# Reloading three chunks' keys, an earlier mask, no unread products, held weights and a new cut of the output in a delta rule with two MoEs

## The chip, the cores and the metric

The kernel runs on one core of one Trainium2 chip. The metric is the time of one execution on the device in microseconds (us); less is better.

## The reference

Three stages follow one another. The first is a recurrence (a delta rule) over 768 time steps for each of 4 batches and 8 heads, with a state of 48 x 48:

```python
k_n = k / (norm(k) + 1e-6)
for t in range(S):
    y[t]  = q[t] @ state
    state = state + beta[t] * outer(k_n[t], v[t] - k_n[t] @ state)
```

Its result, transposed, is a matrix x of 3072 tokens by 384. Two dense layers with a gate (called MoEs in the code) come after it:

```python
h = x @ w_in;  x = (h * tanh(softplus(h))) @ w_out      # first
h = x @ w_in2; out = (h * clip(h + 3, 0, 6) / 6) @ w_out2  # second
```

w_in is 384 x 2048 and w_out 2048 x 384. All is float32.

## The kernel before, in words

**Tiling.** The recurrence is cut into 24 chunks of 32 time steps (`NS`, `C`). All 4 batches x 32 steps of a chunk lie on the 128 partitions. For each chunk the kernel transposes k and q on TensorE (`T_pe`, line 403), forms the matrices of products among its steps (`G_pe`, line 420, masked by VectorE in `G_ew`, `G_ew2`, lines 441 to 451, the first with a mask times beta from `beta_mask`, line 393), solves a triangular system (`quads`, line 575, for chunks 0 to 7; `substs`, line 654, for the rest, on VectorE), and then takes the serial step in `rec` (line 786): products with the state (`state_pe`, L719), the new values (`U_pe`, L729), the output (`MU_pe`, L739), and the state's update (`S_mm`, L769, added by VectorE at L781). In the plan, step t means `rec`'s pass over chunk t; `S<t>` is set when its update is issued on TensorE. `G<t>` is set when the first matrix of one of chunks 0 to 7 is masked, `mt<t>` when the second one is, `n<t>` when the key norms of a chunk are ready.

Tokens go through the MoEs in 6 tiles of 512 (`NB`). For each tile and each of 16 slices of the 2048 inner columns there are 9 products of the first layer (`mm1`, L1084) and, two slices later, 9 or 12 of the second (`mm2_t`, L1105, first MoE; `mm2_second`, L1242, second MoE). Float32 is split into a high and a low part, hence three products for each. The splitting of x is in `make_x` (line 1055, ScalarE L1062, VectorE L1066), that of the weights in `Weights.lane` and `part` (lines 994 and 1034): a lane takes bits apart on VectorE (L1014 to L1029), a part makes the high copy on ScalarE (L1046) and the low one on VectorE (L1049). The first MoE starts when chunks 0 to 3 are through, and it runs between the remaining steps of the recurrence; the second MoE follows when the first is done. The weights of the second are loaded and split from the time the recurrence has ended (`phase2`, line 1264).

**Order.** The kernel is scheduled by hand, through a planner. `Flow` (line 28) runs all these generators as flows on a model of the engines: each `yield (engine, us)` asks for an engine for an estimated time, each `yield "name"` waits for an event of the plan, and of all flows that could go on the one with the least start time plus its penalty (`pen`) is issued next. What comes out is one fixed order of instructions for each engine and for the DMA queues; on the chip the engines follow it in order, with semaphores for the real dependences. `room` (line 204) hands out the accumulator banks. While the recurrence runs beside the first MoE there are five banks; the recurrence's next request, once made, keeps its banks reserved (`chain`), so that an `mm1` gets a bank only when enough others are left.

**What the change touches.** `kp` (line 257) says where a chunk's keys lie: chunks 0 to 4 in `kpad[0..4]`, 5 to 7 in `kx` (a tile that is part of the weight tile `wol3`), later ones in `kpad` in turn. `loads_k` (line 285) loads chunks 8 to 12 after steps 0 to 4, and chunk t from 13 on after step t - 5. `matrices` (line 491) forms the first matrices of chunks 4 to 7, `preps` (line 515) transposes their k and q again and forms the second ones. `masks` (line 540) makes the masks of chunks 8 to 23 on GpSimd. `keep1` (line 1348) holds the low and high parts of the last second-layer weights of the first MoE until their tiles are free. `warm` (line 1384) has two loops of products that nobody reads: one until the first product of the first MoE (L1391), one until the first slice-pass over the first token tile ends (L1399). `flush2` (line 1248) copies a finished tile of the output from the accumulators, alternating ScalarE (L1257) and VectorE (L1255), and stores it (L1259). The two weight lanes of the second MoE have a penalty of 0.2 us (line 1293).

## Time and profile before

| what | before |
|---|---|
| median of 3 runs | 1090.2 us (1089.63 to 1091.22) |
| the profiled execution | 1093.29 us, its span 1091.5 us |
| granted TensorE clock, mean over the span | 0.984 of full speed |
| TensorE busy (matmuls) | 97% of the span, 13342 matmuls |
| VectorE, ScalarE, GpSimd busy | 60%, 39%, 19% |
| chain of work that ended last | TensorE 87%, VectorE 9% |

The span goes from the first to the last instruction of the profiled execution. The engines are TensorE (PE), VectorE (DVE), ScalarE (ACT), GpSimd (POOL) and SyncE (SP, which issues DMAs). "L1084" is line 1084 of the kernel. Matmuls are pipelined: one may begin before the one ahead has ended, and so the difference of two starts tells more than a duration. The granted clock is TensorE's: 1.00 is 2.4 GHz and 0.50 is 1.2 GHz.

### The profile page before, as it was taken

How to read it: one execution, taken by the hardware profiler on the slowest of the kernel's cores; microseconds unless marked ns; L12 is line 12 of the kernel's file. 1: busy time of each engine (PE TensorE's matmuls, PEld its weight loads, DVE VectorE, ACT ScalarE, POOL GpSimd, SP SyncE). 2: the span in 40 equal slices, each digit the busy share in tenths (PEclk: the TensorE clock that was granted, in tenths of full speed). 3: DMA queues.
4: the chain of work that ended last, by engine and by line, in shares of the span. 5: the costliest groups of instructions: out<-in, count | busy, mean ns of one | idle time of the engine just before them, and what ended most of it. 6: DMA issues, size and time to landing. Idle time of an engine off the chain costs nothing.

```text
span 1091.5 us, 30757 instructions
## 1 busy us (share of the span) xinstructions
PE 1063.5 (97%) x13342; PEld 875.3 (80%) x13342; DVE 659.9 (60%) x1553; ACT 420.4 (39%) x823; POOL 204.7 (19%) x215
## 2 busy tenths in 40 slices
PE   8999999999999999999999998999999999999996
PEld 4666786787788788878887886999999999999995
DVE  6778975678496757748671899844343343433432
ACT  4335433443444344344322534433333333433331
POOL 3211341133334233332322332000000000000000
PEclk9999998999999999999999998999999999999998
DMA  6462442222423332241310543401001010010000
GB/s 145 94 158 49 108 114 70 57 72 37 87 41 76 54 70 64 48 76 20 79 22 26 170 134 97 155 1 58 1 3 56 2 59 1 13 45 1 29 1 29
DMA packets 145512, 66.06 MB, mean 61 GB/s; under 512 B 129472, under 2 KB 132544, under 8 KB 145376
## 3 DMA queue, kind: packets, MB, share of 16 engines
q1 hardware_dynamic: 143168, 63.64, 23.8%
q8 instruction: 105, 1.72, 0.7%
q10 hardware_dynamic: 2208, 0.44, 0.2%
q14 instruction: 31, 0.25, 0.1%
HBM read 50.43 MB, written 13.63 MB: 59 GB/s over the span
## 4 chain that ended last, share of the span: by engine, by line
PE 87%; DVE 9%; ACT 1%; issue 1%; DMA 0%; POOL 0%; SPq 0%; ACTq 0%; POOLq 0%; DVEq 0%
PE hps L1084 33%; PE p L1242 18%; PE o L1105 13%; PE warm L1391 4%; PE dsps L769 3%; PE gps L427 2%; PE tps L407 2%; PE ksps L719 2%; PE yps L739 2%; PE ups L729 2%; PE qps L626 2%; DVE cw L1029 2%; PE yps L719 1%; DVE tmp L677 1%; DVE cw L1026 1%; DVE tp L684 1%
## 5 line engine op out<-in xcount | busy, mean ns | idle before, releaser
L1084 PE MATMUL hps<-xh,wih 128*128 128x512 f32 x576 | 230.4, 400 | 5.0 <-ACT g L1115 3.1
L1084 PE MATMUL hps<-xl,wih 128*128 128x512 f32 x576 | 228.2, 396 | 1.1 <-DVE xl L1066 1.1
L1084 PE MATMUL hps<-xh,wil 128*128 128x512 f32 x576 | 227.6, 395 | 0.0
L1124 POOL TENSOR_TENSOR glo<-g,ghi 128x512 fp32r<-128x512 f32 x96 | 129.5, 1349 | 329.4 <-ACT ghi L1090 280.9
L1217 DVE SCALAR_TENSOR_TENSOR r<-r,hps 128x512 f32<-128x512 f32 x96 | 66.0, 688 | 164.6 <-ACT r L1215 164.6
L1215 ACT ACTIVATE r<-hps,half_c 128x512 f32<-128x512 f32 x96 | 66.1, 689 | 171.7 <-PE hps L1084 171.3
L1084 PEld LDWEIGHTS hps<-xh,wih 128*128 128x128 f32 x576 | 108.9, 189 | 28.0 <-ACT g L1115 3.5
L1115 ACT ACTIVATE g<-hps 128x512 f32<-128x512 f32 x96 | 57.1, 595 | 188.1 <-PE hps L1084 188.1
L1242 PE MATMUL p<-woh,glo 128*128 128x384 f32 x384 | 129.5, 337 | 0.0
L1242 PE MATMUL p<-woh,ghi 128*128 128x384 f32 x384 | 129.2, 337 | 0.0
L1242 PE MATMUL p<-wol,ghi 128*128 128x384 f32 x384 | 128.9, 336 | 0.0
L1084 PEld LDWEIGHTS hps<-xh,wil 128*128 128x128 f32 x576 | 109.1, 189 | 23.2
L1084 PEld LDWEIGHTS hps<-xl,wih 128*128 128x128 f32 x576 | 109.0, 189 | 21.8 <-DVE xl L1066 2.8
L677 DVE TENSOR_TENSOR tmp<-tp,ash 128x126 f32<-128x126 f32 (+22 forms) x248 | 100.5, 405 | 39.6 <-DMA ash<-ad 33.0
L1105 PE MATMUL o<-ghi,woh 128*128 128x512 f32 x288 | 113.9, 396 | 0.0
L1105 PE MATMUL o<-ghi,wol 128*128 128x512 f32 x288 | 113.8, 395 | 0.0
L1223 DVE TENSOR_TENSOR glo<-r,ghi 128x512 fp32r<-128x512 f32 x96 | 66.5, 693 | 57.2 <-ACT ghi L1090 56.8
L1090 ACT ACTIVATE ghi<-r 128x512 fp32r<-128x512 f32 x96 | 60.7, 632 | 69.4 <-DVE r L1217 69.4
L781 DVE TENSOR_TENSOR sbd<-sbd,dsps 48x192 f32<-48x192 f32 x152 | 53.5, 352 | 55.2 <-PE dsps L769 52.1
L1105 PE MATMUL o<-glo,woh 128*128 128x512 f32 x288 | 84.3, 394 | 0.0
L684 DVE TENSOR_TENSOR tp<-tp,tmp 128x126 f32<-128x126 f32 (+22 forms) x248 | 77.8, 314 | 7.2
L1242 PEld LDWEIGHTS p<-woh,ghi 128*128 128x128 f32 x384 | 72.2, 188 | 4.0
(138 smaller groups left out, 1448.0 us busy)
## 6 DMA issues: line engine op xcount, KB each, us to landing
raw<-in_moe_w_in_dram SPq DMA_DIRECT2D x24, 512.0 KB
raw<-in_moe_w_out_dram SPq DMA_DIRECT2D x32, 384.0 KB
vt<-in_v_dram SPq DMA_DIRECT2D x96, 48.0 KB
qpad<-in_q_dram SPq DMA_DIRECT2D x96, 48.0 KB
x2d<-x2out SPq DMA_DIRECT2D x6, 768.0 KB
x2in<-x2d SPq DMA_DIRECT2D x6, 768.0 KB
out_dram<-osb SPq DMA_DIRECT2D x24, 192.0 KB
ash<-ad SPq DMA_DIRECT2D x16, 256.0 KB
```

The costliest lines, as they stand in the source:

```text
L677: nc.vector.tensor_tensor(out=tv, in0=x[:, 0:m, j:j + 1].to_broadcast([128, m, n]), in1=a[:, j + 1:C, j:j + 1].rearrange("p i o -> p o i") ...
L684: nc.vector.tensor_tensor(out=x[:, 0:m, j + 1:C], in0=x[:, 0:m, j + 1:C], in1=tv, op=ALU.add)
L781: nc.vector.tensor_tensor(out=o, in0=o, in1=S_part(b, r), op=ALU.add)
L1084: nc.tensor.matmul(out=ps[0], lhsT=w[:, kk, c], rhs=xhl[n][xi][:, kk, :], start=(kk == 0 and x == 0), stop=(kk == KD - 1 and x == 2))
L1090: nc.scalar.activation(out=hi, in_=g, func=ACTF.Copy)
L1105: nc.tensor.matmul(out=acc[i][dc], lhsT=w[:, e, 128 * dc:128 * (dc + 1)], rhs=a, start=(f == 0 and x == 0), stop=(f == KF - 1 and x == 2))
L1115: nc.scalar.activation(out=g, in_=ps, func=ACTF.Mish)
L1124: nc.gpsimd.tensor_tensor(out=lo, in0=g, in1=hi.bitcast(F32), op=ALU.subtract)
L1215: nc.scalar.activation(out=r, in_=ps, func=ACTF.Relu, scale=1.0 / 6.0, bias=half_c)
L1217: nc.vector.scalar_tensor_tensor(out=r, in0=r, scalar=1.0, in1=ps, op0=ALU.min, op1=ALU.mult)
L1223: nc.vector.tensor_tensor(out=lo, in0=r, in1=hi.bitcast(F32), op=ALU.subtract)
L1242: nc.tensor.matmul(out=acc[n][s], lhsT=a[:, c], rhs=w[:, e, :], start=(f == 0 and x == 0), stop=(f == KF - 1 and x == 2))
```

## The change

- Chunks 5 to 7 keep their first load in `kx` for the norms and the first matrices, and are loaded a second time into `kpad[0..2]` after steps 0 to 2, for the second transposes and the state updates. From chunk 5 on all keys lie in the five buffers in turn, so chunk t is loaded after step t - 5.
- The mask of chunk 8 waits in the plan for `G7` instead of `mt7`; the last second-layer weights of the first MoE wait for `G7` instead of `S7`.
- The second loop of unread products is taken out.
- While the second last slice's first-layer products of the first MoE have been planned and the first split of the second MoE's x has not, the weight lanes have a penalty of 2.5 us instead of 0.2.
- The output of a tile is stored by four transfers after all four copies, one for each batch of 32 partitions, instead of one after each copy; on the last tile two of them are issued by ScalarE's queue.

```diff
--- before.py
+++ after.py
@@ -255,10 +255,13 @@
             return flow.landed(2.2)
 
         def kp(t):
-            return kpad[t] if t < 5 else kx[:, t - 5] if t < 8 else kpad[(t - 8) % NKP]
+            return kpad[t % NKP]
+
+        def kp_first(t):
+            return kx[:, t - NKP] if NKP <= t < 8 else kp(t)
 
         def kdata(t):
-            return kp(t).rearrange("p j r d -> p (j r) d")[:, :, 0:D]
+            return kp_first(t).rearrange("p j r d -> p (j r) d")[:, :, 0:D]
 
         def load_k(t):
             flow.ev[f"k{t}"] = load_heads(k, kdata(t), t)
@@ -283,10 +286,12 @@
                     f(t)
 
         def loads_k():
-            for t in range(8, NS):
-                yield f"S{t - 8 if t < 13 else t - NKP}"
+            for t in range(NKP, NS):
+                yield f"S{t - NKP}"
                 yield LOAD
-                load_k(t)
+                flow.ev[f"kk{t}"] = load_heads(k, kp(t).rearrange("p j r d -> p (j r) d")[:, :, 0:D], t)
+                if t >= 8:
+                    flow.ev[f"k{t}"] = flow.ev[f"kk{t}"]
 
         def loads_q():
             for t in range(2, NS):
@@ -400,8 +405,8 @@
             )
             mbs[t] = m
 
-        def T_pe(t, i):
-            src = (kp(t), qpad[t % NQP])[i]
+        def T_pe(t, i, src=None):
+            src = (kp(t) if src is None else src, qpad[t % NQP])[i]
             ps = bank(("T", t, i), [128, NP, 128], "tps")
             for j in range(NP):
                 nc.tensor.transpose(ps[:, j, :], src[:, j].rearrange("p r d -> p (r d)"), ident)
@@ -494,7 +499,7 @@
                 yield f"k{t}"
                 yield room(("T", t, 0))
                 yield "PE", 0.5
-                T_pe(t, 0)
+                T_pe(t, 0, kp_first(t))
                 yield "ACT", 0.6
                 x = ap_.tile([128, NP, B, 1, C], F32, tag=("tp", "an")[t % 2], name="kt")
                 nc.scalar.activation(out=x.rearrange("p j b o s -> p j (b o s)"), in_=tps.pop((t, 0)), func=ACTF.Copy)
@@ -516,6 +521,7 @@
             for t in range(4, 8):
                 yield f"G{t}"
                 yield f"QS{t - NKQ}"
+                yield f"kk{t}" if t >= NKP else "k4"
                 for i in range(2):
                     if i:
                         yield f"q{t}"
@@ -540,7 +546,7 @@
         def masks():
             for t in range(8, NS):
                 yield f"n{t}"
-                yield f"mt{t - 1}"
+                yield f"mt{t - 1}" if t > 8 else "G7"
                 yield "POOL", 0.7
                 beta_mask(t)
                 flow.set(f"mb{t}")
@@ -1255,9 +1261,14 @@
                     nc.vector.tensor_copy(out=o[:, s, :], in_=a[s])
                 else:
                     nc.scalar.activation(out=o[:, s, :], in_=a[s], func=ACTF.Copy)
-                r0 = 128 * i + C * s
-                nc.sync.dma_start(out=out.rearrange("(b n) d -> b n d", b=B)[:, r0:r0 + C, :], in_=o[:, s, :])
             flow.set(f"flush{n}")
+            yield "SP", 0.3
+            for b in range(B):
+                r0 = b * S + 128 * i
+                (nc.scalar if i == NB - 1 and b % 2 else nc.sync).dma_start(
+                    out=out[r0:r0 + 128, :].rearrange("(t s) d -> s t d", s=C),
+                    in_=o[C * b:C * (b + 1)],
+                )
             if i == NB - 1:
                 flow.set("end")
 
@@ -1290,7 +1301,7 @@
                          lambda s: p2.tile([128, 768, 2], U32, tag=s, name="raw2"), tmp, keep)
             flow.add(w2.load())
             for _ in range(2):
-                flow.add(w2.lane(), pen=0.2)
+                flow.add(w2.lane(), pen=lambda: 2.5 if f"mm1.{n + KF - 2}" in flow.ev and f"xk{NB}" not in flow.ev else 0.2)
 
 
         p2 = ps_b = None
@@ -1349,7 +1360,7 @@
 
             g, i = divmod(idx, 7)
             was = {(2, 0): ("wih2", "wil2"), (2, 3): ("wol2",), (3, 0): ("wih3", "wil3"), (3, 3): ("woh3",)}.get((g, i), ())
-            ev = (["sub1"] if g == 3 or (g, i) == (2, 3) else []) + (["S7"] if (g, i) == (3, 3) else [])
+            ev = (["sub1"] if g == 3 or (g, i) == (2, 3) else []) + (["G7"] if (g, i) == (3, 3) else [])
             return ev + [lambda s=s: w1.slots[s] for s in was]
 
         w1 = Weights(1, w1_in, w1_out, ("r0", "r1", "xh", "xl", "wih2", "wil2", "wol2", "wih3", "wil3", "woh3"), raw1,
@@ -1390,14 +1401,6 @@
                 z = ident.bitcast(BF16) if "sub1" in flow.ev else idle
                 nc.tensor.matmul(out=ps[:, 0:z.shape[1]], lhsT=z[:, 0:128], rhs=z, start=True, stop=True)
             release("W")
-            while "mm1.15" not in flow.ev and flow.cur < 300.0:
-                yield "PE", 0.11, 0
-                at, b = min((at, b) if at is not None and b in usable else (1e9, b) for b, at in bank_at.items())
-                if at < flow.cur - 0.5:
-                    held["W"] = b
-                    z = ident.bitcast(BF16)
-                    nc.tensor.matmul(out=bank("W", [128, 256], "warm"), lhsT=z[:, 0:128], rhs=z, start=True, stop=True)
-                    del held["W"]
 
         flow.cur = 1.0
         flow.dma = 9.0
```

## Rows read from the trace of the kernel before

**Rows 1.** The page, its first part: busy us, share of the span, instructions.

```profile
PE 1063.5 (97%) x13342; PEld 875.3 (80%) x13342; DVE 659.9 (60%) x1553; ACT 420.4 (39%) x823; POOL 204.7 (19%) x215
```

**Rows 2.** Busy us by stretch: length, each engine, granted clock, DMA share, GB/s.

```profile
62.50:65.90 3.40, 3.40 (x81) 2.11 (x82) 3.21 (x8) 0.90 (x2) 0.00 (x0) 0.50 0.76 178
...
120.00:160.00 40.00, 40.00 (x847) 31.74 (x849) 33.08 (x80) 16.17 (x34) 17.81 (x14) 1.00 0.38 101
...
178.50:184.10 5.60, 4.84 (x14) 1.36 (x13) 2.20 (x5) 0.34 (x1) 0.00 (x0) 0.50 0.71 177
184.10:188.80 4.70, 4.67 (x101) 3.53 (x101) 0.00 (x0) 0.71 (x2) 0.00 (x0) 0.50 0.00 0
...
227.00:480.00 253.00, 250.72 (x4083) 203.05 (x4083) 182.86 (x528) 104.39 (x236) 89.47 (x90) 1.00 0.32 62
...
672.80:681.60 8.80, 7.69 (x19) 5.17 (x20) 7.78 (x16) 4.00 (x7) 1.39 (x1) 0.61 0.29 95
681.60:1075.00 393.40, 393.40 (x1974) 356.35 (x1974) 163.45 (x261) 141.09 (x224) 0.00 (x0) 1.00 0.09 29
```

**Rows 3.** Line 1399, the second loop's products: durations in ns, first and last start.

```profile
L1399 PE MATMUL warm<-ident x36: 269/270/372, 175.3 to 227.0; 128*128 128x256 bf16 x36
```

**Rows 4.** TensorE in order of time: start, us, instructions; three stretches.

```profile
154.12 0.87 PE L719 MATMUL ksps<-sbd,kqt 128*32 128x96 f32 x32
...
175.31 9.20 PE L1399 MATMUL warm<-ident 128*128 128x256 bf16 x24
184.16 0.78 PE L1084 MATMUL hps<-xh,wih 128*128 128x512 f32 x1
...
201.86 3.55 PE L1399 MATMUL warm<-ident 128*128 128x256 bf16 x11
205.17 0.47 PE L1084 MATMUL hps<-xh,wih 128*128 128x512 f32 x1
```

**Rows 5.** VectorE in order of time, four stretches.

```profile
133.49 2.93 DVE L781 TENSOR_TENSOR sbd<-sbd,dsps 48x192 f32<-48x192 f32 x8
...
177.27 0.47 DVE L451 TENSOR_TENSOR mt<-gps,masku 128x128 f32<-128x128 f32 x2
...
202.44 0.28 DVE L451 TENSOR_TENSOR mt<-gps,masku 128x128 f32<-128x128 f32 x1
...
1081.02 0.56 DVE L1255 COPY osb<-p 128x384 f32<-128x384 f32 x1 [0.49 <-PE p L1242]
```

**Rows 6.** TensorE in order of time at the switch between the MoEs.

```profile
668.91 0.84 PE L1105 MATMUL o<-glo,woh 128*128 128x512 f32 x3
672.85 0.50 PE L1084 MATMUL hps<-xh,wih 128*128 128x512 f32 x1 [3.10 <-ACT g L1115]
...
681.19 0.39 PE L1105 MATMUL o<-glo,woh 128*128 128x512 f32 x1
681.42 0.39 PE L1084 MATMUL hps<-xh,wih 128*128 128x512 f32 x1
```

**Rows 7.** ScalarE in order of time at the switch.

```profile
671.27 0.52 ACT L1046 ACTIVATE woh<-cw 128x384 fp32r<-128x384 f32 x1 [1.69 <-DVE cw L1029]
671.70 0.61 ACT L1062 ACTIVATE xh<-x2in 128x512 fp32r<-128x512 f32 x1
672.22 0.58 ACT L1115 ACTIVATE g<-hps 128x512 f32<-128x512 f32 x1
```

**Rows 8.** SP's DMA issues after 1070 us.

```profile
1079.97 3.08 SPq L1259 DMA_DIRECT2D out_dram<-osb  x4
```

**Rows 9.** DMA from 1070 to 1092 us in 40 slices of 0.55 us: GB/s.

```profile
GB/s 0 0 0 0 0 0 0 0 0 0 0 30 0 0 0 0 0 0 0 0 31 14 47 81 95 101 98 98 98 101 101 101 101 101 101 101 64 0 0 0
```

**Rows 10.** DMA share and GB/s (the last two columns) by stretch: output, stores, loads.

```profile
1083.00:1086.00 3.00, 0.00 (x0) 0.00 (x0) 0.00 (x0) 0.00 (x0) 0.00 (x0) 0.51 0.26 98
...
610.00:614.00 4.00, 4.00 (x19) 3.34 (x18) 3.31 (x6) 2.98 (x5) 1.29 (x1) 1.00 0.93 327
318.50:322.00 3.50, 3.50 (x17) 2.87 (x17) 3.00 (x11) 2.01 (x4) 1.86 (x2) 1.00 0.51 92
```

## The prediction

> **What bounds the kernel now.** I read the page's engine table first, then the busy times by stage, then the instructions in order of time where a stage showed a hole. TensorE is busy 1063.5 us of the 1091.5 us span [rows 1], so a gain can only be TensorE work that goes away, a hole, or time at the lower clock. The windows place them [rows 2]. From 120 to 160 us TensorE works 40.00 of 40.00 us, and from 681.6 to 1075 us 393.40 of 393.40: nothing in these two stretches waits, and moving work inside them gives nothing. From 227 to 480 us 2.3 us of 253 are lost. What remains is three places: 175 to 205 us, the switch between the MoEs at 670 to 682 us, and the end after 1081 us.
>
> Some of what counts as busy is not wanted: 36 products from line 1399 that nobody reads, between 175.3 and 227.0 us [rows 3]. 24 of them stand in one block, 11 in a second [rows 4]. The planner gives each 0.11 us (line 1394), but the block of 24 lasts from 175.31 to 184.16, which is 0.37 us each: every one opens the accumulator bank anew and ends before the next begins. Where the plan saw a hole of some 2.6 us (24 x 0.11) it put 8.85 us of work in order ahead of a useful product.
>
> **The change, part by part. Unread products (removed).** What does the next useful product really wait for? In both places the recurrence has just put four accumulator banks to use for its next step, and the next product must leave four banks free (lines 204 to 224). The last of the four comes free when VectorE ends the two masking instructions of line 451: 177.27 + 0.47 = 177.74 us, and 202.44 + 0.28 = 202.72 us [rows 5]. So without the products TensorE could go on at about 177.8 instead of 184.16 (6.3 us sooner) and at 202.8 instead of 205.17 (2.3 us). The 36th, alone, I set at nothing (0 to 0.4 us). The clock: from 178.5 to 188.8 us the granted clock is 0.50 of full speed, which is 1.2 of 2.4 GHz; in the last 4.7 us of it useful products run [rows 2], and half of that, 2.3 us, is lost. A real hole of 2.4 us stays at 175.4 and may bring a dip of its own; the shortest dip shown is 3.4 us, 62.5 to 65.9 [rows 2], so 1.7 us. Sum: 6.3 + 2.3 + 2.3 - 1.7 = **9.2 us gained**. Bounds: the whole of the two blocks, 8.85 + 3.31 us [rows 4], plus 2.3 of clock, 14.5, if the holes close too; 0 if other waits show up behind them.
>
> **Mask of chunk 8 and keys.** Step 5's first product (line 719) comes at 154.12 us [rows 4], though VectorE has the state of step 4 ready at 133.49 + 2.93 = 136.42 us [rows 5]. In the plan it stands behind the mask of chunk 8, and that behind the matrices of chunk 7. Untied, it may come some 17 us sooner. As TensorE is full in these 40 us, this only exchanges MoE work for recurrence work: 0 us. Cover gone, TensorE would wait in the later stretch for as long as MoE work is missing there. The second transposes of chunks 5 to 7 (line 524) also wait for the reloads, which are issued after steps 0 to 2, long before. Chunks 5 to 7 are loaded a second time. In the SP queue the reloads take the places where chunks 8 to 10 were loaded (after steps 0 to 2), and chunks 8 and 9 those of 11 and 12; what is new are three key loads, 12 issues, after steps 5 to 7. Four issues of SP take 3.08 us at the end, waits included [rows 8]; 3 x 3.1 = 9 us of SP over some 50, with the value and query loads and the last raw weights behind them. They are needed a step later, so 0, and -1 to +1 in the range. The last weights of the first MoE need no longer wait for step 7 (line 1352); TensorE shows no wait for them: 0, and up to 1 us gained.
>
> **Hold at the switch.** The first MoE's last products but nine begin at 668.91 and last 0.84; the next one, the second MoE's first, begins at 672.85, 3.10 us late, behind ScalarE's line 1115 [rows 6]. From 669.75 to 681.42 TensorE does nine products of each MoE, 18 in 11.67 us; at full clock one takes 0.23 us (681.19 to 681.42), so 4.1 us. So 7.6 us are lost, 3.1 by waiting, about 3.4 by the clock (0.61 over 8.8 us [rows 2]), the rest by shorter waits for VectorE's line 1066. The cause is the ScalarE row: the copy of a weight (line 1046) at 671.27 waited 1.69 us for VectorE's weight bits, and behind it in order stood the x copy (671.70) and the activation (672.22) [rows 7]. The new penalty of 2.5 us lets x go first on VectorE for those 6 us or so. After the first MoE's last first-layer products the plan has two groups of second-layer ones, 4.1 us, up to 669.75 (line 1190); x may be overwritten when these begin, and the activation, the x copy (0.58 + 0.61 us) and a split on VectorE of about as long fit in there. **7.0 us gained**; bounds 0 and 7.6. The weights come up to 6 us later; in 393 us after the switch TensorE never waits for them, so 0, and if that cover is gone up to 6 us lost.
>
> **Output.** Before, four transfers of 192 KB go out one by one, each cut into four outermost rows of output. From 1083 to 1086 us 0.26 of 16 engines are busy, that is 4.2, at 98 GB/s; bytes move from 1081.0 to 1090.35 (slices of 0.55 us), 1.0 us after the first issue at 1079.97, and the span ends 1.15 us after the last [rows 8 to 10]. After, all issues wait for the last copy, 1081.02 + 0.56 = 1081.58 [rows 5], and two queues issue two each; bytes from 1082.6. Behind ScalarE's two issues nothing is queued. In the five tiles before, SP waits for the copies once instead of four times, and the x loads behind it have most of a tile's time: 0, by the same 393.40 us. A transfer's outermost side is then 32 rows. Nearest rows: loads of 32 partitions use 0.51 of the engines (92 GB/s, with 192-byte pieces), 768 KB stores of 128 partitions with others 0.93 and 327 GB/s [rows 10]. At 327 GB/s 786 KB take 2.4 us: end at 1082.6 + 2.4 + 0.3 for the second issue + 1.15 = 1086.5, **5.0 us gained**. At 0.51 of 16 engines, 8.2 of them, and 98 / 4.2 = 23 GB/s each, 190 GB/s, 4.1 us: 3.5 gained. At 92 GB/s, 8.5 us: 0.7 lost. I take the first: pieces are 1536 bytes, nearer to the store than to the load.
>
> The Trainium skill, "DMA: Bandwidth & Descriptors", section on why a semaphore rises by 16, says that a transfer runs on the largest number of engines up to 16 that divides the outermost size on both sides: 4 before, as the rows show, and 16 after, which no row here shows for an output. By it the sum is that of 327 GB/s or better; by the row of the loads it would be 1.5 us less.
>
> **Sum.** 9.2 + 7.0 + 5.0 = 21.2 us. The profiled execution took 1093.29 us (span 1091.5), 3.1 above the median of the three timed runs; against the median of 1090.2: 1090.2 - 21.2 = **1069.0 us**.
>
> **Rivals.** (a) The holes are real in full: other waits stand behind the masking, and TensorE idles where the products were. For it: the plan itself saw holes there. Against: VectorE and the banks are ready at 177.74. The first term falls to about 1: 1077 us.
> (b) The clock: TensorE with nothing in a hole falls to 1.2 GHz and stays there for a while, as after the wait of 3.1 us at the switch [rows 2, 6]. Two holes with a dip as long as the longest shown (10.3 us, up to 5.1 lost each) instead of the 1.7 counted: 8.5 more, 1077 us. Against: the longest dip began while the unread products ran, so they did not hold the clock.
> The Trainium skill, "TensorE: Matmul & The Clock Gate", part on what is actually happening, has it that the gate is throttled by default and that activity opens it; that speaks for filling holes, and the dip at 178.5 us under the fillers goes against it here.
> (c) The hold does nothing: it slows the lanes' VectorE work but not the weight copies on ScalarE, which have no penalty. 1090.2 - 14.2 = 1076 us.
> (d) Slower: the reloaded buffers tie steps 5 to 7 to their keys, chunk 7 comes late, and the second block of tokens finds nothing to multiply. A load starts 1.0 us after issue and takes 196 KB / 92 GB/s = 2.1 us; step 5 has 17.7 us in hand (136.42 to 154.12). It decides above 17.7 + 21.2 = 38.9 us over three steps, 13 us a step; at 15 us a step the time is 1096 us.
> (e) Nothing measurable comes of the whole.
>
> **Numbers.** Forecast 0.62, (a) 0.13, (b) 0.08, (c) 0.10, (d) 0.04, (e) 0.03. The forecast's own bounds are 1062 (14.5 + 7.6 + 5.3, and up to 1 for the keys) to 1074 (6 + 6 + 4). (a) to (c) lie at 1076 to 1077, so 1062 to 1078 leaves out less than 2 in 10. About 0.2% (2 us) is what a measurement can tell here: faster 0.93, within it 0.03, slower 0.04.
>
> **What would show it.** No line 1399; between 170 and 205 us waits of TensorE of 1 to 3 us behind line 451 and windows at 1.00 clock; step 5's line 719 near 137 us; at the switch no wait over 0.5 us and 9 + 9 products in about 4.1 us; after the last product bytes over some 0.9 of the engines, and 5 to 6 us instead of 10.5 to the end. I am wrong if TensorE's idle time from 104 to 227 us grows by more than 5 us, if the switch still takes 11 us, or if the output still moves at 100 GB/s.

## The result, and the profile after

The changed kernel takes 1076.46 us (median of four executions, 1072.72 to 1080.24) against 1090.3 us for the kernel before (median of four): a ratio of 0.9868, with a 95% interval of 0.9848 to 0.9889. Five more executions, run later, had a median of 1074.93 us (1073.54 to 1077.5; ratio 0.9860, 0.9837 to 0.9882). The forecast was 1069.0 us with a range of 1062 to 1078: the sign and the range hold, the time came out 7.5 us above the forecast. Two executions in the experiments took 5689.61 and 1271.98 us and are left out below: the profiled one of the changed kernel run again, and one of six of the last version.

The profiled execution took 1080.24 us, the longest of the four, and its span is 1078.5 us. So stages are compared span against span: 1091.5 before, 1078.5 after, 13.0 us less. The page of the changed kernel, its first part and the head of the chain that ended last:

```profile
PE 1049.8 (97%) x13306; PEld 868.1 (80%) x13306; DVE 662.3 (61%) x1553; ACT 420.6 (39%) x823; POOL 205.7 (19%) x215
...
PE 80%; DVE 14%; issue 2%; ACT 1%; DMA 1%; POOL 1%; SPq 0%; DVEq 0%; ACTq 0%; POOLq 0%
```

There are 36 matmuls fewer than in [rows 1], which are the unread products, and TensorE is busy 13.7 us less (1063.5 before). It is still the bound.

The table cuts the span of each profiled execution at starts of TensorE instructions. "Start" ends at the first product of the first MoE, "tile 1" at the first product of the second token tile, "tiles 2 to 6" at the last group of nine first-layer products of the first MoE, "switch" at the second such group of the second MoE, "second MoE" at the end of the last output copy, and "output" at the end of the span.

| kernel | start | tile 1 | tiles 2 to 6 | switch | second MoE | output | span | timed median |
|---|---|---|---|---|---|---|---|---|
| before | 104.6 | 122.8 | 436.1 | 17.95 | 400.2 | 9.93 | 1091.5 | 1090.2 |
| **after** | 107.3 | 111.5 | 441.8 | 11.79 | 400.1 | 6.00 | 1078.5 | 1076.5 |
| difference | +2.7 | -11.3 | +5.8 | -6.2 | 0.0 | -3.9 | -13.0 | |
| before, no unread products | 104.2 | 113.5 | 435.7 | 17.81 | 400.1 | 10.11 | 1081.5 | 1082.9 |
| before, new output cut | 103.3 | 122.7 | 433.4 | 17.61 | 400.1 | 5.82 | 1082.9 | 1087.2 |
| before, hold | 103.6 | 123.5 | 433.5 | 14.71 | 400.2 | 10.11 | 1085.6 | 1085.7 |
| before, keys and masks | 102.5 | 126.5 | 441.0 | 17.97 | 400.2 | 10.19 | 1098.4 | 1100.4 |
| after, old keys and masks | 104.9 | 116.0 | 435.2 | 14.53 | 400.1 | 5.83 | 1076.6 | 1076.8 |
| after, mask tied | 103.8 | 109.2 | 443.1 | 10.94 | 400.1 | 6.01 | 1073.1 | 1077.5 |
| after, old keys, mask untied | 106.0 | 109.9 | 443.5 | 11.72 | 400.1 | 5.82 | 1077.1 | 1076.0 |
| after, steps 13 and 17 moved | 103.7 | 110.7 | 438.3 | 12.34 | 400.1 | 6.00 | 1071.1 | 1072.4 |
| after, no hold | 106.9 | 111.0 | 440.7 | 17.89 | 400.2 | 5.98 | 1082.6 | 1081.4 |
| steps 13 and 17 moved, output in halves | 102.9 | 111.1 | 438.7 | 12.31 | 400.1 | 4.44 | 1069.5 | 1073.1 |
| mask tied, steps 9, 13, 17 moved, halves | 103.8 | 108.2 | 435.7 | 13.11 | 400.1 | 4.36 | 1065.3 | 1069.1 |

One profiled execution tells a stage only to within a few us. The kernel before and the four kernels that keep its keys and masks issue the same TensorE work of the first MoE in the same order, the unread products aside, and their tiles 2 to 6 take 433.4 to 436.1 us; the five with the keys, the mask or both changed and no step moved take 440.7 to 443.5. So the loss in this stage is clear. The start runs from 102.5 to 107.3 us over all rows, and from 102.9 to 107.3 over four kernels whose plan is the same up to there (after, no hold, and the two with only steps 13 and 17 moved); so its +2.7 us is not clear of the spread.

The three terms that were forecast as gains are all there, each within some 2 us of its size. Two stages that were set at nothing grew by 8.4 us together. The busy times by stretch of the changed kernel show where:

```profile
70.50:73.20 2.70, 0.08 (x7) 0.06 (x7) 0.82 (x2) 1.14 (x2) 0.00 (x0) 1.00 0.85 217
74.30:77.70 3.40, 3.40 (x71) 1.64 (x70) 2.35 (x5) 0.22 (x1) 0.00 (x0) 0.50 0.33 57
...
120.00:160.00 40.00, 39.64 (x862) 31.14 (x861) 31.49 (x68) 18.14 (x44) 12.95 (x10) 1.00 0.38 99
...
178.50:184.10 5.60, 5.52 (x123) 4.31 (x114) 4.87 (x11) 3.05 (x10) 2.15 (x5) 1.00 0.77 183
184.10:188.80 4.70, 4.70 (x117) 4.09 (x106) 3.84 (x9) 2.41 (x7) 1.40 (x1) 1.00 0.75 168
227.00:480.00 253.00, 246.46 (x4352) 199.06 (x4353) 175.95 (x514) 104.43 (x241) 88.63 (x91) 0.99 0.33 64
...
672.80:681.60 8.80, 8.80 (x44) 7.75 (x44) 8.14 (x16) 5.28 (x9) 0.00 (x0) 1.00 0.69 229
681.60:1060.00 378.40, 378.40 (x1902) 343.22 (x1901) 149.58 (x233) 133.39 (x212) 0.00 (x0) 1.00 0.08 22
```

Against [rows 2]: the stretch from 178.5 to 188.8 us, at 0.50 of full speed before, is at 1.00 and holds 240 matmuls instead of 115. The nine microseconds after the switch are at 1.00 instead of 0.61. The second MoE is full as before. But from 227 to 480 us TensorE now idles 6.5 us, where it had idled 2.3, and near 70 us it stands still for 2.6 us and then runs 3.4 us at half speed.

### The profile page after: what moved, and what is told of

Same layout as the page of the kernel before. It is cut to its first block, busy times and chain, and to the rows that moved or that the text cites. A ratio compares the mean times of both kernels' runs of the same rounds, so it can differ in the third digit from the quotient of the medians.

```text
span 1078.5 us, 30692 instructions
## 1 busy us (share of the span) xinstructions
PE 1049.8 (97%) x13306; PEld 868.1 (80%) x13306; DVE 662.3 (61%) x1553; ACT 420.6 (39%) x823; POOL 205.7 (19%) x215
## 4 chain that ended last, share of the span: by engine, by line
PE 80%; DVE 14%; issue 2%; ACT 1%; DMA 1%; POOL 1%; SPq 0%; DVEq 0%; ACTq 0%; POOLq 0%
PE hps L1090 31%; PE p L1248 19%; PE o L1111 11%; PE warm L1402 4%; DVE tmp L683 3%; PE dsps L775 3%; DVE tp L690 3%; PE tps L412 2%; PE gps L432 2%; PE yps L745 2%; PE qps L632 2%; PE ups L735 1%; PE ksps L725 1%; PE yps L725 1%; DVE cw L1032 1%
## 5 line engine op out<-in xcount | busy, mean ns | idle before, releaser
L690 DVE TENSOR_TENSOR tp<-tp,tmp 128x126 f32<-128x126 f32 (+22 forms) x248 | 81.9, 330 | 7.4 <-DVE tmp L683 0.5
```

Of the source, the lines that this page charges most:

```text
L690: nc.vector.tensor_tensor(out=x[:, 0:m, j + 1:C], in0=x[:, 0:m, j + 1:C], in1=tv, op=ALU.add)
```

## The experiments

The first four each put one part of the change into the kernel before.

**Unread products alone.** The second loop goes, nothing else.

```diff
-            while "mm1.15" not in flow.ev and flow.cur < 300.0:
...
-                    nc.tensor.matmul(out=bank("W", [128, 256], "warm"), lhsT=z[:, 0:128], rhs=z, start=True, stop=True)
-                    del held["W"]
```

> Kernel before without the second loop of unread products, nothing else. Theory A (the terms of the prediction): 9.2 us less than before, about 1081 us, nearly all of it between the first product of the first MoE and the first product of its second token tile (122.8 us before, about 113 us here); the later tiles as before. Theory B (the products filled real waits; the 11.5 us that this stretch lost in the changed kernel come from the earlier mask and the reloaded keys): 0 to 3 us less, 1087 to 1090 us, the stretch at 120 us or more. Theory C (whatever is taken out of the plan shifts where TensorE runs short of instructions): the stretch shrinks as in A, but the tiles after it grow by 3 to 6 us and the runs spread by several us.

Measured: 1082.9 us (12 executions, 1078.3 to 1090.57), ratio 0.9945 (0.9926 to 0.9963). Tile 1 took 9.3 us less. TensorE in order of time, and the busy times by stretch, of this kernel:

```profile
174.34 0.85 PE L1105 MATMUL o<-glo,woh 128*128 128x512 f32 x3
177.63 0.47 PE L1084 MATMUL hps<-xh,wih 128*128 128x512 f32 x1 [2.44 <-DVE mt L451]
...
195.97 0.47 PE L1084 MATMUL hps<-xh,wih 128*128 128x512 f32 x1 [1.00 <-DVE tp L684]
```

```profile
178.50:182.00 3.50, 3.50 (x101) 3.10 (x101) 2.20 (x5) 0.71 (x2) 0.00 (x0) 0.51 0.77 171
...
184.10:188.80 4.70, 4.70 (x139) 3.89 (x139) 1.54 (x5) 3.10 (x9) 1.97 (x4) 1.00 0.43 94
```

The block of 24 products [rows 4] has become a wait of 2.44 us behind the masking, and the next useful product starts at 177.63 us; the prediction had worked out 177.74. The block of 11 has become a wait of 1.00 us: it is put down to line 684, but the masking of line 451 ends at 195.82 us, 0.15 us before the product, as it does at the first hole. A dip of the clock follows the hole, as the prediction allowed, but of some 3.4 us instead of the 10.3 us under and behind the unread products. So rivals (a) and (b) fall: without the products TensorE goes on 6.5 us sooner in the first place, and the half-speed stretch is shorter without them, not longer.

**The output cut alone.** The hunk of `flush2`, nothing else.

> Kernel before with only the new cut of the output: four transfers after all four copies, one for each 32 partitions, two of the last tile's on ScalarE's queue. Theory A: the time from the last copy's end to the end of the span falls from 9.9 to about 6.0 us as in the changed kernel, so 3.9 us less, about 1086.4 us, and nothing else moves (predicted 5.0). Rival: the five earlier tiles' stores, now issued late and at once, hold up the x loads of the second MoE and part of it is given back: 0 to 2 us less.

Measured: 1087.2 us (12 executions), ratio 0.9977 (0.9962 to 0.9992). From the last copy to the end 5.82 us instead of 9.93, and the second MoE takes 400.1 us as before, so the later stores of the earlier tiles hold up nothing that shows.

**The hold alone.** The penalty of the two weight lanes, nothing else.

> Kernel before with only the penalty of 2.5 us for the weight lanes at the switch. Theory A: from the first MoE's last group of first-layer products to the second group of the second MoE 17.95 us before, about 11.8 here, so 6 us less, about 1084 us, with the half clock at the switch gone. Rival (the switch of the changed kernel got better because the recurrence ended some 17 us earlier and the weight lanes had got further): the switch takes 15 us or more, 0 to 3 us less.

Measured: 1085.72 us (8 executions), ratio 0.9964 (0.9950 to 0.9978). The switch is only 3.24 us shorter. TensorE in order of time there:

```profile
667.79 0.50 PE L1084 MATMUL hps<-xh,wih 128*128 128x512 f32 x1 [0.88 <-ACT g L1115]
...
670.41 0.50 PE L1084 MATMUL hps<-xl,wih 128*128 128x512 f32 x1 [0.95 <-DVE xl L1066]
...
672.26 0.63 PE L1105 MATMUL o<-ghi,woh 128*128 128x512 f32 x1
```

The wait of 3.10 us [rows 6] is 0.88, but a second of 0.95 stands behind the split of x, and the products after it take 0.63 us instead of 0.39: the clock still falls, to 0.51 of full speed from 670.9 to 674.4 us.

**Keys and masks alone.** The hunks of `kp` to `T_pe`, `matrices`, `preps`, `masks` and `keep1`; the loop, the lanes and the output stay as before.

> Kernel before with the reloaded keys, the earlier mask of chunk 8 and the last first-MoE weights tied to G7, but with the loop of products, the old weight penalty and the old output. Theory A (these exchange work, no more): within 2 us of before, 1088 to 1092 us. Theory B: they carry the gain of the first token tile, 8 to 11 us less, about 1080 us, with few of the unread products left. Theory D (they are what makes the later tiles 1 to 3 us longer each, by new waits of TensorE for VectorE's lines 823 and 451): 3 to 6 us more, 1093 to 1096 us.

Measured: 1100.4 us (6 executions), ratio 1.0107 (1.0088 to 1.0126): a part that was set at nothing makes the kernel before 10 us slower, more than any of the three expectations. In the groups of instructions by line the second loop has grown from 36 products [rows 3] to

```profile
L1405 PE MATMUL warm<-ident 128*128 128x256 bf16 x44 | 13.5, 307 | 2.3
```

and 43 of them stand between the state product and the new values of steps 6 and 7. Tile 1 is 3.7 us longer than before, and 15.0 us longer than in the changed kernel, whose order is the same without the products; tiles 2 to 6 are 4.9 us longer than before too, where the loop has long ended. So the loop is one way in which this part costs time, and there is another that has nothing to do with it.

The next four vary the changed kernel.

**Without keys and masks.** The same hunks undone in the changed kernel, all else kept.

> Changed kernel without its key and mask parts: keys, mask of chunk 8 and the tie of the last first-MoE weights as before; no second loop of products, hold and new output cut kept. Theory P (phase: what costs time in the tiles after the first is where a step of the recurrence falls among the MoE's groups; a step with no first-layer products between its line for the state product and its line for the new values leaves TensorE waiting for VectorE): no such step here in the plan, so the five tiles to the first MoE's end take 3 to 6 us less than in the changed kernel, the first tile about 2 more: 1071 to 1075 us. Theory S (the keys and masks are needed for the gain of the first tile when the products are gone): the first tile loses more than that and the time is 1078 us or more.

Measured: 1076.83 us (5 executions, 1071.37 to 1078.32), ratio 0.9847 (0.9821 to 0.9873), the same time as the changed kernel within its spread, and above the 1071 to 1075 us of theory P. The stages are not the same, though: with the keys and masks, tile 1 is 4.5 us shorter (2.0 against the kernel before without the products, which has the same order up to the switch), tiles 2 to 6 are 6.6 us longer and the switch is 2.7 us shorter. "Nothing" is the sum of a gain and a loss. The loss shows in the stretch from 227 to 480 us, which here idles 2.4 us, as before:

```profile
227.00:480.00 253.00, 250.58 (x4178) 203.15 (x4176) 178.26 (x519) 105.03 (x237) 91.01 (x94) 1.00 0.33 65
```

**Only one of the two.** In one kernel the mask of chunk 8 is tied to `mt7` again and the keys stay; in the other the keys and `keep1` are as before and only the mask is untied.

```diff
-                yield f"mt{t - 1}" if t > 8 else "G7"
+                yield f"mt{t - 1}"
```

> Changed kernel with the mask of chunk 8 tied again to chunk 7's matrices, the reloaded keys and the G7 tie kept. Theory P: four steps (9, 13, 17, 21) have no first-layer products between the two lines, 13 and 17 as in the changed kernel, so about the changed kernel's time or 1 to 3 us more, 1076 to 1080 us. Rival (the untied mask alone is what makes the later tiles longer): the later tiles as before the change, 1072 us.

> Changed kernel with the keys and the tie of the last weights as before, the mask of chunk 8 untied. Theory P: steps 9, 13, 17 and 21 without first-layer products, as with the mask tied and the keys reloaded, so 1076 to 1080 us. Rival (the reloaded keys alone make the later tiles longer): 1072 us.

Measured: 1077.45 and 1075.99 us (ratios 0.9866, 0.9846 to 0.9887, and 0.9862, 0.9841 to 0.9883). Both have a tile 1 of 109 to 110 us and tiles 2 to 6 of 443 us. Either edit alone brings both the gain and the loss; the second adds nothing. So it isn't the reloads or the mask as such: what counts is that the recurrence runs earlier among the MoE's groups. Counted in the traces, step 13's state product stands behind 39 groups of first-layer products and three products of the 37th second-layer group in the changed kernel and in both of these; in the kernel before it stands behind 40 and 38 whole groups. TensorE of the changed kernel in order of time, at step 13:

```profile
345.95 1.08 PE L725 MATMUL ksps<-sbd,kqt 128*32 128x96 f32 x32
...
349.02 0.86 PE L1111 MATMUL o<-glo,woh 128*128 128x512 f32 x3
...
351.33 0.88 PE L735 MATMUL ups<-r,pt 32*32 32x48 f32 x64 [1.45 <-DVE r L829]
...
355.80 0.47 PE L1090 MATMUL hps<-xh,wih 128*128 128x512 f32 x1 [1.77 <-DVE mt L456]
```

The state product comes after three of the nine second-layer products of a slice. The other six are issued, and then nothing of the MoE until 355.80: TensorE waits 1.45 us for the new values' inputs and 1.77 us for the masking. In the kernel before the same product stands at the end of such a group, and 18 products of both layers run between it and the new values:

```profile
359.62 0.87 PE L719 MATMUL ksps<-sbd,kqt 128*32 128x96 f32 x32
...
365.99 0.88 PE L729 MATMUL ups<-r,pt 32*32 32x48 f32 x64
...
369.61 0.47 PE L1084 MATMUL hps<-xh,wih 128*128 128x512 f32 x1 [0.92 <-DVE mt L451]
```

Step 17 of the changed kernel stands at the end of a second-layer group, with one such group and no first-layer product before the new values, and waits too:

```profile
445.69 0.91 PE L735 MATMUL ups<-r,pt 32*32 32x48 f32 x64 [0.77 <-DVE r L829]
...
449.71 1.03 PE L412 MATMUL tps<-ident,qpad 128*128 128x128 f32 x4 [1.72 <-issue]
```

The profile names nothing for the second wait; it ends 0.10 us after the first masking instruction of line 456 (449.33 + 0.28 = 449.61 us). Together these are 5.7 us of idle time where the kernel before has 1.5. In all of tiles 2 to 6 TensorE idles 7.9 us instead of 3.3, which is 4.6 of the 5.8 us (the changed kernel first, then the kernel before):

```profile
218.78:660.59 441.81, 433.94 (x6326) 350.87 (x6325) 314.61 (x833) 178.99 (x384) 147.98 (x139) 1.00 0.32 72
```

```profile
227.41:663.47 436.06, 432.81 (x6326) 351.41 (x6326) 307.31 (x814) 176.01 (x377) 142.88 (x138) 1.00 0.30 68
```

A half-speed stretch of 3.4 us stands behind step 17 (449.8 to 453.2 us), but the kernel before has one as long in these tiles (489.1 to 492.6 us). The code suggests why no first-layer product fills in: the recurrence's request keeps banks reserved (`room`, `chain`), and in the middle of a second-layer group no bank is left for the next first-layer one. The next run tests the place; that the banks are the reason no run tests.

**Steps 13 and 17 moved to the end of a group.** In the plan of the changed kernel these two wait for the slice's last second-layer product; no instruction is added.

```diff
+                    if t in (13, 17):
+                        yield f"mm2.{36 if t == 13 else 52}"
                     yield room(("K", t), *([("Y", t)] if t < 4 else []), *([("X", tx)] if tx else []),
```

> Changed kernel in which steps 13 and 17 of the recurrence wait in the plan for the end of the second-layer group that they cut into (groups 36 and 52); nothing else. Theory P: TensorE's idle time at steps 13 and 17 falls from 3.2 and 2.5 us to under 1 each, and with it one dip of the clock: 4 to 6 us less than the changed kernel, 1071 to 1073 us. Rival (what the changed kernel loses there is VectorE's own time, which a later step does not mend): within 1.5 us of the changed kernel, 1075 to 1078 us.

Measured: 1072.39 us (4 executions, 1071.54 to 1073.14), ratio 0.9824 (0.9806 to 0.9843), wholly below the changed kernel's first interval and overlapping its second a little. Tiles 2 to 6 are 3.5 us shorter, and TensorE idles 5.0 us in them instead of 7.9. TensorE in order of time at step 13:

```profile
344.18 0.87 PE L725 MATMUL ksps<-sbd,kqt 128*32 128x96 f32 x32
...
346.25 0.50 PE L1092 MATMUL hps<-xh,wih 128*128 128x512 f32 x1
...
349.19 0.88 PE L735 MATMUL ups<-r,pt 32*32 32x48 f32 x64
...
352.94 0.63 PE L412 MATMUL tps<-ident,qpad 128*128 128x128 f32 x4 [1.49 <-issue]
```

Now three first-layer products get in between and the wait for the new values is gone. A wait of 1.49 us for which the profile names nothing stands a little later, and step 17 still idles 2.2 us (0.49 and 1.71). The 1.49 us, too, end 0.10 us after the first masking instruction of line 456, which VectorE ends at 352.84 us. The code asks for four banks at once for the new values and the transposes behind them, and the masking frees two, so this may be the wait of 1.77 us in another place; no run tests it. So the place among the groups is shown to be a cause. By the table it accounts for 2 to 3.5 of the 5.8 us that tiles 2 to 6 lost (438.3 and 438.7 us in the two kernels with these steps moved, 440.7 and 441.8 in the two with the same plan otherwise); the rest is not settled.

**The changed kernel again, and without its hold.** One kernel is the changed one unaltered; in the other the lanes' penalty is 0.2 again.

```diff
-                flow.add(w2.lane(), pen=lambda: 2.5 if f"mm1.{n + KF - 2}" in flow.ev and f"xk{NB}" not in flow.ev else 0.2)
+                flow.add(w2.lane(), pen=0.2)
```

> The changed kernel once more, unaltered, beside the next three. All theories: 1072 to 1080 us as before. Theory I (the spread of 7 us from execution to execution comes from TensorE running out of instructions at places that vary): the time up to the first product of the first MoE is 107 us if a wait of 2.6 us for nothing that the profile shows stands in step 2's state product, else 103 to 104.5.

> Changed kernel with the weight lanes' penalty at the switch back at 0.2 us. Theory A (the hold is worth what the switch gained, 6.2 us): from the first MoE's last first-layer group to the second MoE's second one 17 to 18 us instead of 11.8, 1082 us. Theory E (part of it comes from the recurrence ending 17 us earlier, so that the weights are further ahead; with the hold alone in the kernel before, the switch took 14.7 us, 3.2 less): the switch takes 14 to 16 us, 2 to 4 us more than the changed kernel, 1079 us.

Measured: 1074.93 us for the first (five executions); its profile is of the execution that is left out, so what it was to tell of the start stays open. 1081.38 us for the second (6 executions), ratio 0.9923 (0.9901 to 0.9945). Without the hold the switch takes 17.89 us, as before. TensorE there:

```profile
667.49 0.50 PE L1090 MATMUL hps<-xl,wih 128*128 128x512 f32 x1 [1.67 <-DVE xl L1072]
...
670.38 0.80 PE L1090 MATMUL hps<-xl,wih 128*128 128x512 f32 x1 [1.92 <-DVE xl L1072]
...
676.09 0.52 PE L1111 MATMUL o<-glo,woh 128*128 128x512 f32 x1
676.45 0.39 PE L1090 MATMUL hps<-xh,wih 128*128 128x512 f32 x1
```

and of the changed kernel, at the same place:

```profile
669.08 0.50 PE L1090 MATMUL hps<-xl,wih 128*128 128x512 f32 x1 [0.94 <-DVE xl L1072]
...
672.16 0.39 PE L1111 MATMUL o<-glo,woh 128*128 128x512 f32 x1
672.39 0.39 PE L1090 MATMUL hps<-xh,wih 128*128 128x512 f32 x1
```

Two waits of 3.6 us together and products of 0.63 us from 671 to 676 us become one wait of 0.94 at full clock: the hold is worth 6.1 us at the switch beside the rest of the change, and 4.9 or 6.5 us of time against the two medians of the changed kernel, where alone it is worth 3.2 and 4.5.

**Two versions beyond the change.** The first adds to the moved steps an output of the last tile in two halves: four transfers after the second copy, four after the fourth. The second takes the tied mask with the new keys, moves steps 9, 13 and 17 and has the halves too.

```diff
+                if i == NB - 1 and s == 1:
+                    store(0, 2, (nc.sync,) * B)
...
+            if i == NB - 1:
+                store(2, 4, (nc.scalar, nc.scalar, nc.sync, nc.scalar))
+            else:
+                store(0, 4, (nc.sync,) * B)
```

> Changed kernel with steps 13 and 17 held to the end of a second-layer group, and the last tile's output in two halves: four transfers of 64 of each batch's rows after the second copy, four after the fourth. From the last copy's end to the end of the span 6.0 us in the changed kernel; if the rate of transfers from 32 partitions is the limit (about 200 GB/s alone, 300 with two at once), half of the bytes are gone before the last copy's issue and 4.2 to 4.8 us remain; if the fixed cost of issue and landing is, 5.5 or more. In all 1070 to 1071.5 us.

> The kernel with reloaded keys but the mask of chunk 8 tied again (whose first tile was the shortest, 109.0 us), with steps 9, 13 and 17 held to the end of the second-layer groups 21, 37 and 53, and the output's last tile in halves. Theory P (the phase of the steps is what the later tiles lose by): the tiles from the second on take 436 to 439 us instead of 443, the first 109, 1068 to 1071 us in all. Rival (the tiles' sum is fixed by VectorE): 442 us or more, 1073 us.

Measured: 1073.13 us (five executions; ratio 0.9845, 0.9823 to 0.9868) and 1069.08 us (five, 1066.68 to 1074.38; 0.9819, 0.9789 to 0.9849). The halves bring the end from 6.0 to 4.4 us in both profiles, but the first version's time isn't below the moved steps alone and misses the 1070 to 1071.5 us expected. The second is the fastest median of all; its span in the profile is 1065.3 us, with tiles 2 to 6 at 435.7, as in the kernel before, and step 13 behind 38 second-layer groups again. It beats the kernel before beyond doubt; its interval overlaps that of the changed kernel a little, so that it beats that one too is likely and not certain.

## Why the prediction was right or wrong

**Unread products: right.** Forecast 9.2 us; 9.3 us of tile 1 when done alone (1082.9 against 1090.2 timed, 7.3 us), 6.8 in the changed kernel without keys and masks, where a second half-speed stretch (116.1 to 119.6 us) takes some of it, and 11.3 in the changed kernel with the earlier recurrence. The wait that the prediction found behind line 451 was there, within 0.3 us of the place worked out. In the changed kernel it isn't: between 107 and 227 us the only wait of TensorE over 0.5 us is one of 1.17 us before 201.36 us, for which the profile names nothing and which ends 0.10 us after the first masking of line 456 (200.97 + 0.29 us), and the dip of 10 us has gone altogether. That the recurrence, moved forward, leaves more MoE work ready there is argued, not shown. "Waits of 1 to 3 us behind line 451" was thus right for that part alone, and of little use as a sign in this kernel.

**Mask and keys: the net was right, the step was not.** "As TensorE is full in these 40 us, this only exchanges MoE work for recurrence work: 0 us." Step 5's state product did move:

```profile
142.66 0.87 PE L725 MATMUL ksps<-sbd,kqt 128*32 128x96 f32 x32
```

That is some 5 us later than forecast, of which 2.7 are the late start of the first MoE. The step took moving inside a full stretch for free; that waits might show up later for want of cover it did say, and set them at nothing. What it left out is that an earlier recurrence lands at other places among the MoE's groups, for the rest of the first MoE: 2.0 to 4.5 us gained in tile 1, 6.6 lost in tiles 2 to 6, 2.7 gained at the switch. That the three nearly cancel is luck of this plan; with the unread products still there the same hunks cost 10 us. Rival (d), late loads, isn't what made that kernel slower: its steps 5 to 7 come at 137.6, 164.4 and 190.9 us, all earlier than before (154.1, 171.7 and 199.0).

**Hold: nearly its size, but not by the hold alone.** Forecast 7.0, measured 6.2 at the switch. One wait of 0.94 us for the split of x stayed, where "no wait over 0.5 us" was forecast. Rival (c) is refuted by the run without the hold. But alone the hold gave less than half: 3.24 us, and 3.42 in the changed kernel without keys and masks. In the changed kernel the recurrence and the weights that follow it are ahead at the switch. In the profiles with the hold the switch is the shorter, the longer the last step's state product lies ahead of it: 10.9 to 11.8 us where it begins 91 to 92 us after that product, 12.3 where 82, 13.1 to 14.7 where 76 to 77. That this lead is why the terms are more than additive goes with these rows, but no run varies it alone.

**Output: the rate was mis-sized.** Forecast 5.0, measured 3.9 by the profile of the changed kernel and 4.1 alone, some 3 us timed. SP's and ScalarE's issues, the DMA slices from 1069 to 1079 us (0.25 us each) and the busy times after the last copy:

```profile
1072.59 0.79 SPq L1268 DMA_DIRECT2D out_dram<-osb  x2
1072.60 0.86 ACTq L1268 DMA_DIRECT2D out_dram<-osb  x2
```

```profile
GB/s 0 0 0 0 0 0 0 0 0 0 0 0 0 0 0 0 0 74 203 197 197 197 191 197 160 178 289 307 276 240 227 184 31 0 0 0 0 0 0 0
```

```profile
1074.00:1076.00 2.00, 0.00 (x0) 0.00 (x0) 0.00 (x0) 0.00 (x0) 0.00 (x0) 0.61 0.92 214
```

0.92 of 16 engines are busy, but they move 214 GB/s, 14.5 for each busy one, where the large stores of [rows 10] moved 327 at 0.93. The prediction took the price of a store over 128 partitions for one over 32; the value it had kept as the lower end, 190 GB/s and 3.5 us, was nearer. (With the 0.3 us of the second issue, which its first sum has, its two lower sums come to 3.3 us gained and 1.1 lost, not 3.5 and 0.7.) The Trainium skill, "DMA: Bandwidth & Descriptors", section on why a semaphore rises by 16, gives 16 engines for an outermost side of 32; the row agrees, with 0.92 of the 16 busy. A full set of busy engines didn't mean a full rate here.

**The start: not foreseen, and not the change's.** 2.7 us of the profiled execution lie before the first MoE. In order of time TensorE of the changed kernel:

```profile
69.98 0.54 PE L725 MATMUL ksps<-sbd,kqt 128*32 128x96 f32 x16
73.14 0.54 PE L725 MATMUL ksps<-sbd,kqt 128*32 128x96 f32 x16 [2.62 <-issue]
```

and of the kernel with the moved steps, whose plan is the same up to here:

```profile
70.06 0.87 PE L725 MATMUL ksps<-sbd,kqt 128*32 128x96 f32 x32
```

TensorE stops in the middle of a series of 32 alike products, and waits for nothing that the profile shows. The same stop of 2.5 to 2.8 us is in four other profiles, among them the kernel before without its second loop; in the rest it is 1.0 us or less, or absent. So it isn't the change. Nor is it the whole of the 2.7 us: the last version has the stop and a start of 103.8 us, the kernel without the hold only 1.0 us of it and a start of 106.9. What else makes up the spread of this stage stays open.

**The sum.** By the stages of the profile: +2.7 - 11.3 + 5.8 - 6.2 - 3.9 us, which is -13.0 before rounding, against the -21.2 forecast. Of the 8.2 us missing, 5.8 are tiles 2 to 6, 2.7 the start, 1.1 the output and 0.8 the hold, less 2.1 that tile 1 gave beyond its term. The three gains come to 21.4 us together, as forecast, but only with the keys and masks that were set at nothing: without them the same three stages gain 6.8 + 3.4 + 4.1 = 14.3 us. So that they add up to the forecast is in part luck as well. The time lies outside the forecast's own bounds, 1062 to 1074 us; the range held since it reached to the rivals at 1076 and 1077 us. The time is theirs, but not by what they say.

## What to carry to other kernels

In a kernel with one fixed order on every engine, "the engine is full here" prices an exchange of work only for that stretch: look where the moved chain lands for the rest of the plan, which products stand between a serial step's request and its answer, and whether a bank is free for others in between. Filler work that the plan prices at 0.11 us and the chip at 0.37 costs more than the hole it fills. And take a transfer's rate from a row with the same number of partitions; a busy share of the DMA engines isn't a rate.

## What the runs showed of the hardware that was not expected

Short waits don't decide alone whether the clock falls. 1.45 and 1.77 us of waiting around step 13 brought no dip (the granted clock from 345 to 356 us is 1.00), 0.77 and 1.72 us around step 17 did (0.50 from 449.8 to 453.2 us), and 0.88 and 0.95 us at the switch did in the kernel with the hold alone. Even the same waits do it in one execution and not in another: the kernel without the hold has the same order there, waits 0.79 and 1.76 us around step 17, and keeps the full clock:

```profile
444.00:456.00 12.00, 9.43 (x251) 7.69 (x251) 9.52 (x39) 4.74 (x14) 3.67 (x3) 1.00 0.29 52
```

A 32-partition store that runs alone moved about 200 GB/s on some 14 busy engines (191 GB/s and 0.90 of 16 from 1073.50 to 1075.25 us). The last two run side by side from 1075.25 us on: they begin at 289 and 307 GB/s and fall to 184 (the slices above), 217 on average over 2 us. So two at once move hardly more than one alone.

The stop of 2.6 us goes with an instruction transfer that comes late. From the DMA queues of the changed kernel from 70.5 to 71.5 us, and of the kernel with the moved steps from 67 to 70.5 us, the instruction queue:

```profile
q8 instruction: 1, 0.02, 6.8%
```

```profile
q8 instruction: 1, 0.02, 1.7%
```

From 67 to 70.5 us the changed kernel has none, while its loads keep 16 engines 88% busy. The Trainium skill, "Runtime: NRT & Kernel Launch", section on instruction fetch mechanics, says that an engine's instructions come in blocks of 16 KiB by a queue of its own while it executes, and that crossing a block is mostly hidden; the trace agrees with the size (104 transfers, 1.70 MB in this queue), and the 2.6 us would be a case that isn't hidden. The other profiles bear this out: in all 13, the seventeenth of the 32 products starts no sooner than 2.3 us after such a transfer has begun, and in the nine where it waits 0.4 us or more it starts 2.4 to 2.7 us after (70.66 and 73.14 us in the changed kernel; 67.02 and 69.44 in the first version with the halves, where it waits 0.42 us). So the wait is as long as the transfer is late. This is a relation in time; no run moves a transfer, so the cause isn't shown by experiment, and what makes the transfer late stays open. It may be a part of why executions of one kernel lie up to 7.5 us apart.
